# A hand-ordered attention and token-mixing kernel: the first batches' transfers in another sequence and every operation in a new order

## The chip, the cores and the metric

The kernel runs on one core of a Trainium2 chip. The core has TensorE (PE, matrix products into the eight banks of PSUM), VectorE (DVE), ScalarE (ACT), GpSimd (POOL, which cannot read PSUM) and SyncE (SP). Sixteen DMA engines move data between HBM and SBUF; POOL, SP and ACT each issue transfers on a queue of their own. The metric is the device time in microseconds, and smaller is better.

## The reference

Eight batches of eight heads, 576 positions, 64 columns a head; `p` has 32 rows a head. Everything arrives in float32.

```python
def sm_attn(qq, kk, vv):
    s = scale * np.matmul(qq, kk.transpose(0, 1, 3, 2))
    a = np.exp(s - np.max(s, axis=-1, keepdims=True))
    a = a / (np.sum(a, axis=-1, keepdims=True) + 1e-09)
    return np.matmul(a, vv)
p_packed = sm_attn(p, k, v)              # 32 rows attend to 576
x = sm_attn(q, p_packed, p_packed)       # 576 rows attend to 32
# heads side by side: x is (8, 576, 512)
W = scale2 * np.einsum("bsd,btd->bst", x @ w_q, x @ w_k)
out = np.maximum(np.einsum("bst,btd->bsd", W, x), 0.0) @ w_out
```

## The kernel before

**The order is written out by hand.** The text `SCHEDULE` (lines 11 to 60) is a list of some 650 items, and the last loop of the kernel emits them one after the other. An item `name@b` is one operation for batch `b`; behind it may stand the engine of an eviction or reduction (`s` ACT, `v` DVE, `g` POOL), the form of a product (`f` whole, `c` split into two halves of 64 columns), and behind a colon the PSUM bank or banks. Each engine takes its own items in the order of the list, and waits at each for what that item needs: its inputs, and the release of the bank or buffer that it overwrites. Nothing is reordered when the kernel runs. A transfer of POOL also waits until the transfer eight places earlier on that queue has landed, since its completion counter is one of eight used in turn.

**Loads.** `LQ`, `LK`, `LV` (line 149, POOL) bring q, k or v of one batch, 1.18 MB in float32, and cast it to bf16 on the way (576 KB). `PB` (line 180, POOL) brings `p` of all batches, `PF` (line 167, ACT) that of the first alone. The k of batch 0 comes on another path, in float32, through SP: `KA` and `KB` (line 170) bring half each into `k_f`, and `cA0` to `cB1` cast it on DVE or ACT. `cw0` to `cw3` (line 279) bring the two small mixing weights, `wo0`, `wo1` (line 288) the output weights. `id` builds the identity matrix for transposes on POOL.

**One batch, in the order of its data:**

- `kt0`, `kt1` (line 305, batch 0: `kf0` to `kf3`, line 258) transpose k by head on PE, `ke0`, `ke1` (batch 0: `kfe0` to `kfe3`) evict it into `kT`. `tp`, `lp` and `tr`, `lq0`, `lq1` do the same for `p`.
- `s0` (line 346) forms the first scores in three banks; `nm0` takes the maximum on DVE, `ex0` and `ex1` the exponentials on ACT (line 360) with their sums, `rc1` the reciprocal of these, `rm` (line 409, POOL) spreads it over a mask.
- `xt0`, `xt1` (line 377) transpose the exponentials, `xe0`, `xe1` evict them. `pv` (line 422) multiplies by v, `pp` (line 431) normalizes, `pt` and `pte` transpose and evict the packed rows.
- `qt0`, `qt1` with `qe0`, `qe1` do for q what `kt` does for k. `e0`, `e1`, `e2` (lines 471, 484) form the second scores. Their softmax goes one of two ways: batches 0 to 3 take `mn` (maximum), `ea` (it is added on PE, line 540) and `xa` (exponential), batches 4 to 7 `mx`, `sb` and `x0`. `sm0` sums, on DVE or, in five steps, on POOL, `rr0` inverts, `ml0` to `ml2` (line 576) multiply.
- `at0`, `at1` (line 596) transpose the weights, `ae0`, `ae1` evict them into `a2T`. `pq`/`pqe`, `wk`/`wke`, `wz`/`wkx`, `wq`/`wqe`, `g`/`ge`, `y`/`ye` are the small products of the mixing and their evictions.
- `m0`, `m1`, `m2` (lines 740, 765) mix, `r00` to `r11` and `r2` are the ReLUs, `o0` to `o4` (line 782) the output projection, `oe0` to `oe4` its evictions into `o_sb` and `ox`, and `st0` to `st2` (lines 812, 816, SP) the stores. `o_sb` has two slots for each half, so an eviction two batches later waits for the store.

`w1`, `w2` (line 204) multiply zeros into a bank, to keep PE occupied while it has nothing to do. Several batches are in work at a time: while PE projects batch `b`, the loads of batch `b + 4` and later arrive.

## Time and profile before

| | us |
|---|---|
| median of 3 runs | 118.99 (118.69 to 119.18) |
| the profiled execution | 119.33 |
| its span, first to last instruction | 117.6 |
| PE busy | 106.7 (91%) |
| DVE busy | 88.7 (75%) |
| ACT busy | 88.8 (76%) |
| POOL busy | 56.4 (48%) |
| filling products of PE (`w1`, `w2`) | 9.8 |

A row of the chain of waits or of the timeline gives a start and a length in microseconds, counted from the first instruction. PE's products are pipelined, so that the length of one is more than the distance to the next. A group's row gives the number of instructions, their busy time and mean in nanoseconds, and the idle time of the engine before them with what ended it. A row of DMA packets gives their number, the MB that they wrote, and their time as a share of sixteen engines.

### The profile page before, as it was taken

How to read it: one execution, taken by the hardware profiler on the slowest of the kernel's cores; microseconds unless marked ns; L12 is line 12 of the kernel's file. 1: busy time of each engine (PE TensorE's matmuls, PEld its weight loads, DVE VectorE, ACT ScalarE, POOL GpSimd, SP SyncE). 2: the span in 40 equal slices, each digit the busy share in tenths (PEclk: the TensorE clock that was granted, in tenths of full speed). 3: DMA queues.
4: the chain of work that ended last, by engine and by line, in shares of the span. 5: the costliest groups of instructions: out<-in, count | busy, mean ns of one | idle time of the engine just before them, and what ended most of it. 6: DMA issues, size and time to landing. Idle time of an engine off the chain costs nothing.

```text
span 117.6 us, 4918 instructions
## 1 busy us (share of the span) xinstructions
PE 106.7 (91%) x2134; PEld 70.1 (60%) x2134; DVE 88.7 (75%) x174; ACT 88.8 (76%) x172; POOL 56.4 (48%) x83
## 2 busy tenths in 40 slices
...
GB/s 62 373 206 207 209 207 208 189 207 208 208 209 205 209 207 209 207 209 207 209 206 211 220 329 241 212 198 377 380 165 112 66 8 233 308 89 307 381 355 117
DMA packets 18069, 25.47 MB, mean 217 GB/s; under 512 B 2176, under 2 KB 14720, under 8 KB 18048
## 3 DMA queue, kind: packets, MB, share of 16 engines
q0 software_dynamic: 13920, 14.49, 73.4%
...
## 4 chain that ended last, share of the span: by engine, by line
PE 59%; DMA 28%; ACT 3%; POOL 3%; issue 1%; DVE 1%; SPq 1%; POOLq 0%; ACTq 0%; DVEq 0%
PE psum L782 24%; DMA v_sb<-in_v_dram 20%; DMA out_dram<-o_sb 8%; PE psum L305 8%; PE psum L740 4%; PE psum L422 3%; PE psum L686 3%; PE psum L596 2%; PE psum L471 2%; PE psum L654 2%; PE psum L377 2%; PE psum L540 2%; PE psum L709 1%; ACT o_sb L136 1%; PE psum L438 1%
## 5 line engine op out<-in xcount | busy, mean ns | idle before, releaser
L782 PE MATMUL psum<-w_out,r 128*64 128x512 bf16 (+2 forms) x240 | 31.9, 373 | 0.5 <-ACT o_sb L136 0.5
L576 POOL TENSOR_TENSOR a<-e,rr 128x512 bf16<-128x512 f32 (+1 forms) x19 | 16.0, 866 | 9.1 <-DVE rr L572 4.1
L782 PEld LDWEIGHTS <-r 128*64 128x64 bf16 (+1 forms) x240 | 13.3, 109 | 11.0 <-issue 2.6
L136 ACT ACTIVATE o_sb<-psum 128x512 f32<-128x512 f32 (+1 forms) x25 | 14.4, 587 | 5.0 <-PE psum L782 4.2
L360 ACT ACTIVATE e1T<-psum,nmax 128x576 bf16<-128x576 f32 x16 | 11.7, 739 | 2.2 <-DVE nmax L356 2.2
L136 ACT ACTIVATE kT<-psum 128x1280 bf16<-128x1280 bf16 (+2 forms) x8 | 8.5, 1080 | 5.2 <-PE psum L305 4.9
L356 DVE TENSOR_REDUCE nmax<-psum 128x2 f32<-128x1152 f32 x8 | 10.8, 1355 | 2.1 <-PE psum L346 1.9
L305 PE MATMUL psum<-ident,q_sb 128*64 128x128 bf16 x288 | 10.4, 220 | 2.1 <-DMA q_sb<-in_q_dram 2.1
L136 ACT ACTIVATE r<-psum 128x512 bf16<-128x512 f32 x20 | 10.7, 610 | 0.8 <-PE psum L740 0.8
L204 PE MATMUL psum<-zero 128*64 128x512 bf16 (+1 forms) x39 | 9.8, 497 | 1.3 <-DVE zero L183 1.2
L305 PEld LDWEIGHTS <-q_sb 128*64 128x64 bf16 x288 | 8.5, 110 | 3.8 <-DMA q_sb<-in_q_dram 2.6
L565 POOL TENSOR_TENSOR rt<-e 128x576 f32<-128x576 f32 x4 | 5.7, 1416 | 8.6 <-ACT e L556 7.9
L305 PE MATMUL psum<-ident,k_sb 128*64 128x128 bf16 x252 | 9.1, 220 | 0.0
L149 POOL DMA_DIRECT2D v_sb<-in_v_dram x8 | 6.1, 767 | 5.7 <-DMA v_sb<-in_v_dram 2.9
L305 PEld LDWEIGHTS <-k_sb 128*64 128x64 bf16 x252 | 7.9, 110 | 1.0 <-issue 0.2
L138 DVE TENSOR_SCALAR r<-psum 128x512 bf16<-128x512 f32 x12 | 7.9, 683 | 0.6 <-PE psum L740 0.6
L149 POOL DMA_DIRECT2D q_sb<-in_q_dram x8 | 6.2, 779 | 4.6 <-PE psum L305 2.3
L142 DVE COPY qT<-psum 128x1280 bf16<-128x1280 bf16 (+1 forms) x10 | 7.5, 751 | 0.6 <-PE psum L305 0.4
L142 DVE COPY o_sb<-psum 128x512 f32<-128x512 f32 x8 | 5.5, 687 | 3.0 <-ACT o_sb L136 2.2
L136 ACT ACTIVATE e<-psum 128x512 bf16<-128x512 bf16 (+1 forms) x10 | 6.3, 639 | 1.1 <-PE psum L377 1.1
L149 POOL DMA_DIRECT2D k_sb<-in_k_dram x7 | 5.4, 770 | 3.6 <-DMA k_sb<-in_k_dram 3.0
L142 DVE COPY kT<-psum 128x1024 bf16<-128x1024 bf16 (+3 forms) x10 | 6.6, 662 | 0.6 <-PE psum L305 0.3
...
## 6 DMA issues: line engine op xcount, KB each, us to landing
...
```

What stands on the lines that cost most here:

```text
L136: nc.scalar.activation(dst, src, func, scale=scale)
L138: nc.vector.tensor_scalar(dst, src, 0.0, None, op0=MAX)
L142: nc.vector.tensor_copy(dst, src)
L149: nc.gpsimd.dma_start(t.rearrange("p g j d -> p g (j d)"), src[b].rearrange("(g h2) (sp j) d -> (h2 sp) g (j d)", h2=2, j=NJ),)
L204: nc.tensor.matmul(bank(ks[0])[r], zero[:, r], zero, start=True, stop=True, skip_group_check=True,)
L305: nc.tensor.transpose(tp[64 * g2:64 * g2 + 64, gp, :, 64 * (j - j0):64 * (j - j0) + 64], S_[b][src][:, gp + 2 * g2, order[j]], ident,)
L356: nc.vector.tensor_reduce(tile("nmax", [P, 2], fp32, b), S_[b]["s1"], axis=AX, op=MAX, negate=True)
L360: nc.scalar.activation(tile("e1T", [P, NJ, 2, 64], bf16, b)[:, :, h2], S_[b]["s1"][:, h2].rearrange("a (j s) -> a j s", j=NJ), EXP, bias=S ...
L565: nc.gpsimd.tensor_tensor(t, e[:, :, 0:16], e[:, :, 16:32], op=ADD)
L576: (nc.gpsimd if on == "g" else nc.vector).tensor_tensor(tile("a2", [P, NU, L], bf16, b)[:, r], S_[b]["e2"][:, r], S_[b]["rr"][:, r].to_bro ...
L740: nc.tensor.matmul(S_[b]["m", gp, h2], S_[b]["y"][r, 128 * gp:128 * gp + 128], S_[b]["wqT"][r, :], start=True, stop=True,)
L782: nc.tensor.matmul(ps[r, 0:w.stop - w.start], src[:, i, r], w_out[:, i, w], start=(i == 0), stop=(i == 3),)
```

## The change

The list is replaced as a whole; it has the same operations for every batch.

- At the start POOL issues `LQ@0` first, then `PB`, `LV@0`, `LK@1`, `LK@2`, and builds the identity only then; `LQ@1` and `LV@1` follow, and the weights `cw0` to `cw3` come behind `LV@1`. From `LK@3` on the loads have the order that they had. SP issues `KA` ahead of `KB`.
- 47 evictions and other operations move from ACT to DVE and 39 the other way; two multiplications move from DVE to POOL and one back. 26 products change between whole and split form, and most change their banks.
- The filling products are 28 pieces instead of 26, at other places of the list's first third.
- Among the operations of the middle, the order between batches changes by a few places throughout. The functions gain an operation that takes the three second scores of a batch in one step (`mn6`, `ea6`, `xa6`, `mx6`, `sb6`), which the new list doesn't use, and `e2` may be given no bank, which isn't used either.

The two lists, up to the point that the prediction follows, and the code:

```diff
-    id@0 PB@0 w1@0c:1 LQ@0 w1@0c:0 w1@0c:0 w1@0c:5 PF@0 LV@0 w1@0c:7 w1@0c:1 KB@0 LK@1 w2@0c:2
-    pfc@0s LK@2 w1@0c:1 cB0@0v KA@0 LQ@1 cB1@0v w1@0c:2 cA1@0s w1@0f:3 kf2@0:7 kfe2@0v w1@0c:3 cw1@0
-    kf3@0:1 cA0@0v tp@0:7 lp@0s w1@0f:6 kf0@0:0 kfe3@0v cw0@0 cw2@0 kfe0@0v kf1@0:3 kfe1@0s tr@0:76
-    lq1@0s cw3@0 s0@0:3 qt0@0:2 w1@0f:0 w1@0f:0 nm0@0 ex0@0 ex1@0 w1@0f:6 lq0@0s qt1@0:0 xt0@0c:4
-    xt1@0f:3 w1@0f:5 rc1@0 qe1@0v w1@0f:0 LV@1 rm@0 xe0@0v w1@0f:7 xe1@0s pv@0:3 qe0@0v w1@0c:0 pp@0
-    pt@0c:2 pte@0v e0@0c:4 kt1@1:1 ke1@1s mn0@0 e2@0:3 mn2@0 kt0@1:0 ke0@1v e1@0c:7 w1@0f:5 mn1@0
-    LK@3 LQ@2 ea2@0c LV@2 s0@1:0 ea0@0c LK@4 xa2@0 ea1@0f xa0@0 w1@0c:5 nm0@1 xa1@0 sm0@0v wo1@0
-    ex0@1 kt1@2:3 wo0@0 rr0@0 ml0@0v ex1@1 w1@0f:5 kt0@2:7 ke1@2s ke0@2s qt1@1:5 ml1@0v qe1@1v
-    xt0@1c:1 qt0@1:2 xt1@1c:0 LV@3 xe1@1v rc1@1 rm@1 ml2@0v at0@0f:4 qe0@1s w1@0f:3 s0@2:5 at1@0f:3
-    pq@0:2 xe0@1v ae0@0s pv@1:0 nm0@2 ae1@0s pqe@0s ex0@2 wk@0f:2 wz@0 pp@1 pt@1c:0 pte@1v LQ@3
-    wq@0:1 wkx@0 ex1@2 e1@1f:0 e0@1f:5 mn0@1 e2@1:7 mn2@1 wke@0s g@0f:2 ge@0v wqe@0s xt1@2f:4
-    xt0@2f:6 ea0@1c mn1@1 xe1@2s kt1@3:2 xe0@2v LK@5 xa0@1 ea2@1f xa2@1 ea1@1f xa1@1 ke1@3v pq@1:6
-    rc1@2 y@0:4 ye@0v pqe@1s kt0@3:1 ke0@3s rm@2 w1@0f:2 m1@0:45 sm0@1v rr0@1 ml1@1g r11@0s qt1@2:2
-    qe1@2s qt0@2:1 qe0@2v s0@3:5 pv@2:1 r10@0s ml0@1g nm0@3 m0@0:04 pp@2 pt@2f:1 r00@0v ex1@3
-    at0@1f:2 pte@2v ml2@1g ex0@3 r01@0v LQ@4 at1@1f:3 e1@2f:1 e0@2f:0 ae0@1s LV@4 mn1@2 ae1@1s LK@6
-    e2@2:6 mn2@2 kt0@4:7 kt1@4:4 ke1@4s LQ@5 ke0@4v mn0@2 wk@1f:3 wz@1 wke@1v wkx@1 wq@1:2 ea2@2c
-    rc1@3 rm@3 xa2@2 ea1@2c xa1@2 pq@2:7 pqe@2s wqe@1v ea0@2c xa0@2 s0@4:3 xt0@3f:6 xe0@3s xt1@3f:1
-    xe1@3s nm0@4 g@1f:2 sm0@2v rr0@2 o3@0f:7 LK@7 ml1@2g ge@1s ml2@2v ex1@4 ex0@4 rc1@4 o2@0f:0
-    ml0@2g o0@0c:2 oe0@0v LV@5 oe3@0s y@1:3 pv@3:5 LV@6 pp@3 ye@1s xt0@4f:1 xe0@4v m1@1:34 r11@1v
-    rm@4 oe2@0s m0@1:27 r00@1v qt0@3:0 qt1@3:5 r10@1s xt1@4c:4 r01@1s xe1@4s pt@3c:7 pte@3v LQ@6
-    at1@2f:2 m2@1f:1 qe1@3v at0@2f:7 qe0@3s o1@0f:4 ae0@2s e1@3f:3 e0@3f:6 r2@1v kt1@5:0 ae1@2v
-    pq@3:5 mn1@3 mn0@3 e2@3:2 mn2@3 oe1@0s pqe@3v ea1@3c kt0@5:7 LQ@7 ea0@3f ea2@3f ke1@5s xa1@3
-    ke0@5v xa0@3 wk@2f:4 wz@2 qt1@4:0 wq@2:3 wke@2v wkx@2 qe1@4v s0@5:5 g@2f:4 xa2@3 sm0@3g wqe@2s
-    qt0@4:0 ge@2s y@2:3 ye@2s nm0@5 ex0@5 ex1@5 qe0@4v pv@4:1 pp@4 o2@1c:3 rr0@3 m0@2:01 oe2@1s
-    m1@2:24 r11@2s ml0@3g pt@4f:5 r10@2s r01@2s pte@4v o1@1f:6 e1@4f:5 e0@4f:4 r00@2v at0@3f:0
-    ae0@3s oe1@1v mx0@4 xt0@5f:2 e2@4:6 xe0@5s kt0@6:1 pq@4:3 pqe@4s ke0@6s mx2@4 o0@1c:0 ml1@3g
-    kt1@6:2 oe0@1s mx1@4 ml2@3g sb2@4 st0@1 qt1@5:6 xt1@5f:1 at1@3f:0 sb1@4 sb0@4 x0@4 ae1@3s ke1@6v
-    s0@6:3 rc1@5 qe1@5v sm0@4g o4@1f:2 xe1@5s wk@3f:0 kt0@7:1 nm0@6 ex1@6 kt1@7:6 wz@3 rm@5 oe4@1v
-    ke0@7v wkx@3 ke1@7v qt0@5:2 wq@3:1 ex0@6 rc1@6 wke@3s qe0@5s pv@5:3 s0@7:5 rr0@4 pp@5 xt0@6f:2
-    pt@5f:3 ml0@4g wqe@3s nm0@7 xt1@6f:4 g@3f:0 LV@7 o3@1f:1 pte@5s e0@5f:3 ge@3v xe0@6s ml1@4g
-    o2@2f:2 e1@5f:0 ex0@7 xe1@6v ml2@4g at1@4f:4 mx0@5 ex1@7 at0@4f:5 sb0@5 oe3@1s y@3:6 mx1@5
-    e2@5:3 rm@6 st1@0 oe2@2s ye@3s ae0@4s xt0@7c:1 rc1@7 rm@7 mx2@5 sb1@5 sb2@5 ae1@4v xe0@7s
...
+    LQ@0 PB@0 KA@0 cA1@0v w1@0c:0 KB@0 w1@0c:0 w2@0f:1 LV@0 w1@0c:0 w2@0c:3 PF@0 pfc@0v w1@0c:7 LK@1
+    LK@2 id@0 w1@0c:3 w1@0f:7 cB0@0s cB1@0v kf1@0:6 kfe1@0v w1@0c:3 w1@0c:1 kf3@0:4 kfe3@0s kf2@0:7
+    w1@0f:5 cA0@0v kf0@0:6 tp@0:5 lp@0s kfe2@0v kfe0@0v s0@0:5 w1@0f:4 w1@0f:4 w2@0f:2 nm0@0 ex1@0
+    ex0@0 qt1@0:0 LQ@1 tr@0:34 lq0@0v xt0@0f:6 LV@1 xt1@0f:5 qt0@0:7 rc1@0 rm@0 xe1@0v xe0@0s pv@0:5
+    cw2@0 cw0@0 cw1@0 w1@0c:2 pp@0 w1@0c:2 pt@0f:5 cw3@0 w1@0f:2 w1@0c:2 pte@0v w1@0c:6 qe1@0s
+    qe0@0s e1@0c:5 mn1@0 kt0@1:0 kt1@1:2 lq1@0s LK@3 ea1@0c ke0@1v w1@0c:4 xa1@0 e2@0:7 e0@0c:6
+    ke1@1v s0@1:3 LQ@2 mn0@0 ea0@0c mn2@0 xa0@0 ea2@0f nm0@1 w1@0f:2 xa2@0 kt1@2:6 w1@0c:2 kt0@2:1
+    sm0@0v LV@2 rr0@0 ex1@1 ex0@1 xt1@1f:3 rc1@1 rm@1 ke1@2v qt0@1:2 qe0@1v ml1@0g xe1@1v qt1@1:4
+    w1@0f:6 ml2@0v xt0@1f:7 LK@4 xe0@1v ke0@2s s0@2:0 nm0@2 qe1@1s at1@0f:3 ex0@2 ml0@0g w1@0f:4
+    ex1@2 pv@1:5 pp@1 pq@0:7 pt@1c:5 ae1@0v at0@0f:4 pte@1v e0@1f:6 ae0@0v mn0@1 wo1@0 e1@1f:3 mn1@1
+    wo0@0 xt0@2f:2 LV@3 LQ@3 pqe@0s wk@0f:7 e2@1:5 wz@0 wkx@0 wke@0v ea0@1c kt1@3:0 LK@5 mn2@1
+    ke1@3v xe0@2s xa0@1 kt0@3:4 g@0f:7 ea2@1f xa2@1 pq@1:6 pqe@1s ea1@1c xa1@1 wq@0:0 wqe@0s
+    xt1@2c:5 xe1@2s rc1@2 ge@0v y@0:1 qt1@2:6 rm@2 ke0@3v ye@0v sm0@1v rr0@1 m0@0:43 r00@0v w1@0c:5
+    ml2@1g qe1@2s s0@3:0 ml1@1g nm0@3 r01@0s qt0@2:5 qe0@2s m1@0:67 r11@0s pv@2:3 ex1@3 pp@2 pt@2f:3
+    pte@2v ex0@3 at1@1f:4 r10@0v ml0@1g at0@1c:7 e0@2f:3 e1@2f:5 LQ@4 mn0@2 mn1@2 kt0@4:2 kt1@4:0
+    ke1@4v ea0@2f ae0@1s ae1@1s wk@1f:4 e2@2:7 wz@1 wke@1v mn2@2 ke0@4s ea1@2c s0@4:0 xt1@3c:6 xa0@2
+    ea2@2c xa1@2 wq@1:3 wkx@1 LV@4 xe1@3s xa2@2 xt0@3f:4 wqe@1s g@1f:5 ge@1s nm0@4 ex1@4 ex0@4
+    o2@0f:7 o3@0f:6 LK@6 oe3@0s xe0@3v rc1@3 sm0@2v rr0@2 pv@3:3 LQ@5 LK@7 LV@5 rm@3 oe2@0s pp@3
+    y@1:0 ye@1s pq@2:2 ml1@2v pqe@2s o0@0c:5 oe0@0s ml2@2v pt@3c:3 m1@1:64 r10@1v m0@1:02 rc1@4
+    at1@2c:1 qt0@3:5 r01@1s LV@6 r00@1s qt1@3:6 xt1@4f:0 r11@1s ae1@2v xt0@4c:2 ml0@2g qe0@3v
+    m2@1f:4 LQ@6 rm@4 pte@3s at0@2f:5 qe1@3v e0@3f:6 e1@3f:7 mn1@3 xe1@4s kt1@5:0 xe0@4s e2@3:3
+    kt0@5:2 mn0@3 ae0@2s ea1@3c r2@1s mn2@3 wq@2:5 ea0@3c ke0@5s xa1@3 ke1@5v xa0@3 wqe@2v wk@2f:4
+    wz@2 s0@5:0 wkx@2 ea2@3c xa2@3 o1@0c:7 wke@2v oe1@0s pq@3:4 qt1@4:5 nm0@5 qt0@4:3 qe1@4v pqe@3s
+    qe0@4v LQ@7 g@2f:7 pv@4:5 pp@4 ge@2s sm0@3g ex0@5 y@2:3 ye@2v ex1@5 o2@1f:7 oe2@1s rr0@3 ml2@3g
+    ml0@3g pt@4f:5 pte@4v m0@2:30 r00@2v m1@2:12 r10@2s e1@4f:4 mx1@4 r01@2s xt0@5f:5 e0@4f:7 xe0@5v
+    mx0@4 r11@2s sb1@4 rc1@5 ml1@3g o1@1f:6 oe1@1s kt1@6:0 e2@4:3 mx2@4 rm@5 ke1@6s sb0@4 kt0@6:2
+    pq@4:5 pqe@4s o0@1f:4 at0@3f:7 sb2@4 x0@4 qt0@5:3 qe0@5s sm0@4g ke0@6v s0@6:0 ae0@3v qt1@5:5
+    xt1@5f:7 qe1@5s oe0@1v st0@1 at1@3f:4 nm0@6 ex1@6 ae1@3v xe1@5v o4@1f:3 oe4@1v kt1@7:4 ke1@7v
+    rr0@4 ml0@4g ex0@6 rc1@6 kt0@7:6 ml2@4g ke0@7v ml1@4g wq@3:3 xt1@6f:0 pv@5:4 pp@5 xt0@6c:7
+    xe0@6v LV@7 st1@0 xe1@6s s0@7:0 nm0@7 wqe@3s pt@5c:4 pte@5s at0@4f:3 ae0@4s wk@3f:7 e2@5:4 wz@3
+    e0@5f:5 wke@3s ex1@7 o3@1f:6 ex0@7 mx2@5 e1@5f:3 wkx@3 rm@6 sb2@5 g@3f:7 ge@3s o3@2f:4 at1@4f:7
+    mx0@5 oe3@1s xt0@7f:0 o2@2f:6 mx1@5 sb1@5 oe3@2s xe0@7s ae1@4v sb0@5 y@3:3 ye@3v pv@6:1 wk@4f:5
...
@@ -476,9 +476,9 @@
         S_[b]["e", i] = ps.rearrange("s (u l) -> s u l", l=L)
 
     @op
-    def e2(b, ks):
-        S_[b]["e2bank"] = ks[0]
-        ps = bank(ks[0])[:, 0:128]
+    def e2(b, ks=None):
+        S_[b]["e2bank"] = ks[0] if ks else S_[b]["ebank", 0] + 2
+        ps = bank(S_[b]["e2bank"])[:, 0:128]
         for gp in range(2):
             for h2 in range(2):
                 nc.tensor.matmul(
@@ -490,7 +490,12 @@
 
     EU = EU + ((0, 32),)
 
+    def whole(b):
+        S_[b]["e", 6] = bank(S_[b]["ebank", 0], fp32, 3)[:, 0:NU * L].rearrange("s (u l) -> s u l", l=L)
+
     def units(i, t):
+        if i == 6:
+            return t
         if i >= 4:
             return t[:, 0:32].rearrange("s (x g) l -> s g x l", g=2)[:, i - 4]
         return t[:, EU[i][0]:EU[i][1]]
@@ -498,6 +503,8 @@
     def emax(i, b):
         if i == 3:
             S_[b]["e", 3] = bank(S_[b]["ebank", 0], fp32, 2).rearrange("s (u l) -> s u l", l=L)
+        if i == 6:
+            whole(b)
         nc.vector.tensor_reduce(units(i, tile("mx", [P, NU, 1], fp32, b)), S_[b]["e", i], axis=AX, op=MAX)
 
     def esub(i, b):
@@ -522,13 +529,15 @@
                             S_[b]["ppT"][r, h2, gp, 32 * g2:32 * g2 + 32], start=True, stop=True,
                         )
 
-    for i in range(6):
+    for i in range(7):
         if i < 2:
             ops[f"e{i}"] = lambda b, md, ks=None, i=i: scores(i, b, md, ks)
         ops[f"mx{i}"] = lambda b, i=i: emax(i, b)
         ops[f"sb{i}"] = lambda b, i=i: esub(i, b)
 
     def nmax2(i, b):
+        if i == 6:
+            whole(b)
         nc.vector.tensor_reduce(
             units(i, tile("mn", [P, NU, 1], bf16, b)), S_[b]["e", i], axis=AX, op=MAX, negate=True)
 
@@ -545,6 +554,13 @@
     def exps(i, b):
         nc.scalar.activation(units(i, tile("e2", [P, NU, L], fp32, b)), S_[b]["e", i], EXP, scale=scale)
 
+    def shifts(b, md):
+        for i in range(3):
+            shift(i, b, md)
+
+    ops["ea6"] = shifts
+    ops["mn6"] = lambda b: nmax2(6, b)
+    ops["xa6"] = lambda b: exps(6, b)
     for i in range(3):
         ops[f"mn{i}"] = lambda b, i=i: nmax2(i, b)
         ops[f"ea{i}"] = lambda b, md, i=i: shift(i, b, md)
```

34 lines of the change are left out of this document (17 added, 17 removed).

## The prediction

> **What bounds the kernel now.** I read the chain that ended last first, then a table by stages, then PE's waits, then POOL's issues and their landings.
>
> ```profile
> 14.62 12.44 DMA v_sb<-in_v_dram
> ...
> 38.94 1.20 PE psum L305 x36
> ...
> 41.74 0.60 PE psum L346 x8
> ...
> 64.04 9.37 DMA out_dram<-o_sb
> ...
> 73.48 0.61 ACT o_sb L136
> ```
>
> In this chain (start, length, what) LV@1, issued at 14.62, lands at 27.06, and pv@1 follows at 27.11, where the first stage of the next table ends. From there the chain is mostly PE's, but for a store that holds an o_sb slot until 73.4, for which the eviction at 73.48 waited.
>
> ```profile
> 14.48:27.11 12.63, 10.13 (x244) 7.22 (x245) 9.97 (x18) 7.98 (x13) 6.43 (x10) 1.00 1.29 203
> 27.11:38.94 11.83, 10.99 (x262) 8.19 (x262) 10.48 (x21) 10.53 (x23) 6.55 (x9) 1.00 1.22 207
> 38.94:58.50 19.56, 19.56 (x411) 13.51 (x412) 17.84 (x34) 16.76 (x35) 11.84 (x16) 1.00 1.21 208
> 58.50:74.20 15.70, 15.08 (x312) 10.90 (x311) 14.99 (x29) 13.90 (x28) 10.52 (x15) 1.00 1.18 239
> 74.20:113.30 39.10, 39.10 (x753) 24.01 (x752) 27.26 (x55) 31.65 (x59) 13.21 (x19) 1.00 0.66 225
> ```
>
> Columns: stage, length, then busy time of PE, weight loads, DVE, ACT, POOL, granted clock, DMA share, GB/s. The clock is 1.00 throughout, and the DMA engines are full (share over 1) up to 74 us. PE idles 2.5 us between pv@0 (14.48) and pv@1, 0.8 up to kt0@4 (38.94), nothing up to 58.5, 0.6 up to 74.2, and nothing in the 39 us behind that. PE's useful work is the same in both kernels (wide and split forms of a product take the same time in the chain), so the end moves by what happens before about 74 us: by when PE comes to a point, and how much of its list it has done by then. DVE and ACT are nearly as full as PE from 27 to 74 us.
>
> PE's own waits behind 38.94 are one row:
>
> ```profile
> PE psum L782 <- ACT o_sb L136: 0.5, 1, 0.5
> ```
>
> That is the projection which waited for the eviction of 73.48 to 74.09, which waited for the store's slot.
>
> **The change part by part.**
>
> *Loads.* The order of LQ, LV and LK is kept; PB falls behind LQ@0, and the four small cw transfers move from ahead of LV@1 to behind it. These rows are POOL's issues of PB, LQ@1, cw3, LV@1 and LK@4, then the times from issue to landing of LQ@1, cw3 and LK@4:
>
> ```profile
> 1.43 0.73 POOL L180 DMA_DIRECT2D p_b<-in_p_dram  x1
> ...
> 5.09 0.83 POOL L149 DMA_DIRECT2D q_sb<-in_q_dram  x1
> ...
> 11.13 0.61 POOL L279 DMA_DIRECT2D wqk<-in_moe_w_k_dram  x1 [2.27 <-DMA q_sb<-in_q_dram]
> 14.62 0.75 POOL L149 DMA_DIRECT2D v_sb<-in_v_dram  x1 [2.88 <-DMA v_sb<-in_v_dram]
> ...
> 24.33 0.75 POOL L149 DMA_DIRECT2D k_sb<-in_k_dram  x1
> ```
> ```profile
> DMA to landing us min/median/max: 18.2/18.2/18.2
> ```
> ```profile
> DMA to landing us min/median/max: 13.1/13.1/13.1
> ```
> ```profile
> DMA to landing us min/median/max: 14.6/14.6/14.6
> ```
>
> LQ@1 lands at 23.3, cw3 at 24.2, LK@4 at 38.9: without the weights ahead of it LV@1 comes 0.9 earlier, at 26.1, and the weights at 27.1, before pq@0 wants them. LK@3 and all that follow have the same bytes ahead of them as before, so they land when they did: LK@4 at 38.9, where kt0@4 stood ready in the old kernel. POOL's issue now waits for the transfer eight places earlier, as LV@1 did above (2.88 for LV@0), but always with two loads or more in the queue; I cost that at nothing, as cover is some 6 us.
>
> *The start.* id goes behind five issues, so LQ@0 is issued at about 0.73 instead of PB at 1.43. ident is then ready at about 5, still ahead of its first use (k_f lands at 5.1). Whether the earlier issue gains or harms depends on how it shares with the two k_f transfers of SP:
>
> ```profile
> q1 hardware_dynamic: 91, 0.21, 108.7%
> ```
>
> This is the whole of what moved from 5.0 to 5.5 (packets, MB, share of the engines): SP's queue alone. PB, issued at 1.43, had moved nothing 4.1 us later, with the engines full of k_f. With the same lag LQ@0 moves at 4.8. By then some 0.3 to 0.4 MB of k_f are left (0.21 of it in this half microsecond), 0.9 us for k_f alone. Shared evenly, k_f's second half lands up to 0.9 later; queued behind, not at all. I take +0.5, and for the range 0 and what an even share from 2.6 us on would cost (rivals). The Trainium skill's page DMA: Bandwidth & Descriptors (Issuing engines are not separate DMA queues) says that DMAs of several engines interleave on the same 16, so that starting one earlier saves only issue time; by it too the earlier start gains no bandwidth, and the row of full engines agrees.
>
> *Front, batch 0.* The rows are a cast of k_f behind its second landing and two kT evictions:
>
> ```profile
> 6.67 0.49 DVE L142 CAST k_sb<-k_f 128x640 bf16<-128x640 f32 x1
> 7.08 0.42 DVE L142 COPY kT<-psum 128x512 bf16<-128x512 bf16 x1
> 7.73 0.49 DVE L142 COPY kT<-psum 128x640 bf16<-128x640 bf16 x1 [0.23 <-PE psum L258]
> ```
>
> DVE now runs cB1, kfe1 and then cA0 after the second landing, though cA0's data came at 5.1: 6.67 + 0.49 + 0.42 + 0.49 = 8.07, then kf0's ten transposes (7.21 to 7.68 in the old order, between these rows) and kfe0, 0.49: s0@0 at about 9.3 where the old order could have it at 8.9, +0.4. pv@0, then, is held by its own evictions instead of LV@0: about 14.6, +0.1. Behind it there is a gain: rm@0 no longer stands behind LV@1's issue on POOL (14.62 to 15.37, then rm@0's own time), so pp@0 is 0.7 earlier, and batch 0's scores with it. Through kt@1, s0@1, nm0@1 and ex@1 this shrinks, since xt1@1 waits for both exponentials: nm0@2 starts at 26.35 as before and pv@1 at about 26.9 (-0.2), with at0@0 and pq@0 (0.34 us) not yet done. The 0.9 of LV@1 is thus mostly not used: pv@1's other input, xe0@1, is there at 26.1 at best, and PE has s0@2 and at1@0 ahead of it.
>
> *27 to 42 us, where the order decides.* Between nm0@2 and pp@2 DVE loses xe0@2 and qe0@2 and gains ae1@0, ae0@0, wke@0, ke0@3 and r00@0. Means from the groups by shape:
>
> ```profile
> L142 DVE COPY qT<-psum 128x1024 bf16<-128x1024 bf16 x5 | 3.4, 688 | 0.4 <-PE psum L305 0.4
> ...
> L142 DVE COPY kT<-psum 128x1024 bf16<-128x1024 bf16 x4 | 2.8, 692 | 0.3 <-PE psum L305 0.3
> ...
> L142 DVE COPY a2T<-psum 128x768 bf16<-128x768 bf16 x4 | 2.2, 550 | 0.7 <-PE psum L599 0.7
> L142 DVE CAST wk<-psum 128x256 bf16<-128x256 f32 x5 | 2.1, 418 | 0.2 <-ACT e L546 0.2
> ...
> L142 DVE COPY e<-psum 128x640 bf16<-128x640 bf16 x4 | 1.9, 482 | 0.0
> ```
>
> 0.55 (ae1, 768 columns) + 0.42 (ae0, taken as wk's) + 0.42 (wke) + 0.69 (ke0) + 0.69 (the ReLU, taken as qT's copy) - 0.48 (xe0) - 0.69 (qe0) = +1.6 us, in a stage where DVE idles 11.83 - 10.48 = 1.35. It is full, and pp@2 ends 0.2 to 0.6 later; I take 0.4 (37.7 for 37.3). nm0@3 ahead of it is late as much, ACT's ex1@3 and ex0@3 follow, and kt0@4, written into banks that ex0@3 reads, waits for them to 39.35 instead of LK@4 at 38.9. ACT then has ae0@1, ae1@1 and ke0@4 before s0@4: at about 41.5, where the old kernel had it at 41.6. By then the new list lacks wq@1, ea2@2 and pq@2 (0.44 + 0.06 + 0.11 = 0.6 us of PE, start to start). Net +0.5, and a full PE does not win that back.
>
> *42 to 76 us.* Followed through with the same durations, PE finds its inputs in time; small waits at pv@4 and s0@7 add 0.2. The wait of 0.5 on that eviction goes: o3@2 uses bank 4, which PE wants only at m0@3, two us later. But oe0@1 is late on DVE, so st0@1 and st1@0 are issued about 1 us later than 64.04 and the slot comes free at 74 to 75; y@3 is what waits then, by 0 to 1. I take -0.3 in all (-0.5 to +0.7).
>
> *Behind 76 us* PE has the same products; evictions move between DVE and ACT, which have 11.8 and 7.4 us to spare there (39.10 less 27.26 and 31.65). I take 0; the last evictions and stores are the same pieces as before.
>
> Sum: +0.5 (start) +0.5 (27 to 42) -0.3 = +0.7 us on the profiled execution's 119.33. That lies 0.34 above the median of 118.99; against the median it is 119.7.
>
> **The rivals.**
>
> *The loads run ahead (faster).* If the engines have room at the start, all of the stream, LK@4 too, lands earlier by what the first issue gains, 1.43 - 0.73 = 0.7; with half the forecast's gain behind 42 us (-0.3), and DVE keeping up, the time is 118.99 - 1.0 = 118.0. For it: what PE does up to 58 us hangs on landings. Against: PB's 4.1 us of waiting on full engines, and DVE's full stage, which does not follow the loads. It decides if kt0@4 starts before 38.6.
>
> *The parts cancel (no change).* k_f is not disturbed, and the 0.5 lost up to 42 us is paid by the 0.5 of that one wait: 119.0.
>
> *LQ@0 breaks into k_f (clearly slower).* While both queues have work they take turns:
>
> ```profile
> q1 hardware_dynamic: 244, 0.93, 61.6%
> q0 software_dynamic: 301, 0.33, 48.2%
> ```
>
> From 67 to 71 stores and loads move about packet for packet. If LQ@0's packets don't wait as PB's did, but come while k_f has only begun, at about 2.6, then nearly 1 MB of k_f shares half and half from there, the second half lands 2.4 later, and the chain s0@0, nm0@0, ex, pv@0, pp@0, s0@1, pv@1 moves with it: 118.99 + 0.2 + 2.4 = 121.6. It decides from a k_f landing behind 7.5. Against it: PB had its descriptors written at 2.16 and took no turn until 5.5. The Trainium skill's page DMA: Bandwidth & Descriptors (Queues, rings and completion order) has each DMA engine go round its queues packet by packet; by that rule this rival is what happens, the rows of 67 to 71 agree with it, and those of PB don't.
>
> **How the numbers follow.** A run tells 0.5% (0.6 us) from no change. The forecast's case (start and DVE cost, little gained back, 119.2 to 120.6) has 0.40, of which 0.13 lies within 0.5%; cancelling 0.20; loads ahead 0.24; LQ@0 into k_f 0.16. So faster 0.24, same 0.20 + 0.13 = 0.33, slower 0.27 + 0.16 = 0.43. The range goes from 118.1, within the faster case, to 121.3, near the end of the slowest; some 0.1 is left out on either side. The forecast's own range is 119.2 to 120.6.
>
> **What would show it.** LV@1 landing at 26.1 with pv@1 still at 26.7 or later, behind s0@2 and at1@0; k_f's second landing between 6.6 and 7.5; DVE without idle time from 26 to 38; kt0@4 behind ex0@3 and not behind LK@4; s0@4 at 41.3 to 42.3; no wait of L782 on an o_sb eviction about 74, but one of L725 there. The prediction is wrong if pv@1 starts before 26.4 and kt0@4 with LK@4's landing, if that landing itself moves from 38.9, or if PE has a wait of over 0.5 us behind 76, where I expect none.

## The result and the profile after

The changed kernel takes 119.9 us (median of 14 runs, 118.94 to 120.15) where before takes 119.01 (14 runs on the same chip, 118.57 to 120.44): a ratio of 1.0059, with a 95% interval of 1.003 to 1.0087. It is slower by about 0.6%, and the 119.7 of the prediction lies 0.2 below it. The profiled execution took 119.78, with a span of 118.0; that of before took 119.33 and 117.6. The granted clock was 0.992 to 1.000 in the changed kernel's 14 runs, the short ones and the long ones alike, so it is not what spreads them.

At four points TensorE has done the same set of operations in both kernels: ahead of `kt0@4` (but for `e2@2`, 0.06, which the changed kernel still has to do there), `o2@1`, `pv@6` and `y@6`/`y@7`. Between them the lengths can be compared directly. These are the tables of stages with the boundaries at these points, first before, then the changed kernel. The columns are the stage, its length, and then busy time and instructions of PE, weight loads, DVE, ACT, POOL, the granted clock, the DMA share and GB/s.

```profile
38.94:56.72 17.78, 17.78 (x396) 12.75 (x397) 16.69 (x32) 14.98 (x31) 10.81 (x13) 1.00 1.21 208
56.72:75.12 18.40, 17.78 (x336) 12.01 (x333) 16.91 (x34) 16.61 (x34) 11.63 (x18) 1.00 1.19 235
75.12:101.60 26.48, 26.48 (x626) 17.64 (x624) 19.71 (x41) 23.85 (x43) 13.13 (x18) 1.00 0.64 207
```
```profile
39.46:57.56 18.10, 17.95 (x419) 12.91 (x417) 16.35 (x29) 16.05 (x35) 10.77 (x14) 1.00 1.21 208
57.56:75.10 17.54, 17.54 (x325) 11.67 (x325) 17.10 (x35) 15.13 (x31) 10.60 (x16) 1.00 1.18 236
75.10:102.11 27.01, 26.60 (x631) 17.77 (x632) 22.84 (x50) 21.36 (x37) 13.75 (x19) 1.00 0.65 212
```

The changed kernel comes to `kt0@4` 0.52 later (39.46 for 38.94), loses 0.32 more up to `o2@1`, takes 0.86 less up to `pv@6`, where both are level (75.10 and 75.12), and loses 0.53 behind that. The sum is +0.51, and the time is +0.45.

PE's waits behind 27 us, in the changed kernel:

```profile
PE psum L438 <- DVE pp L431: 1.5, 2, 0.9
PE psum L422 <- issue: 0.4, 1, 0.4
```

The first row is `pt@1` and `pt@2`, which wait for DVE's `pp`. The wait of 0.5 on an o_sb eviction is gone, as forecast. The second row is new. "Issue" means that PE waited for nothing that the trace shows, and it lies behind 76 us, where I expected nothing. First the changed kernel, then before at the same operation:

```profile
83.91 0.28 PE L422 MATMUL psum<-v_sb,e 64*64 64x128 bf16 x7
84.59 0.60 PE L422 MATMUL psum<-v_sb,e 64*64 64x128 bf16 x29 [0.41 <-issue]
```
```profile
84.42 0.70 PE L422 MATMUL psum<-v_sb,e 64*64 64x128 bf16 x36
```

In the changed kernel `pv@7` stops after 7 of its 36 products.

The front, in the chain of waits, the last rows ahead of the full stage of DVE:

```profile
25.46 0.77 DVE a L592
26.25 0.48 DVE e L142
26.72 0.95 DVE nmax L356
```

LV@1 landed at 26.29 (before 27.07) and PE began `pv@1` at 26.87 (before 27.11), so LV@1 no longer holds PE. What stands ahead of `nm0@2` is a multiply of the softmax, `ml2@0` (line 592, which is 576 in before). The timeline shows it on DVE beside one of POOL, then the same place in before:

```profile
25.11 1.05 POOL L592 TENSOR_TENSOR a<-e,rr 128x512 bf16<-128x512 f32 x1
25.38 0.94 DVE L592 TENSOR_TENSOR a<-e,rr 128x128 bf16<-128x128 f32 x1
```
```profile
25.75 0.27 DVE L576 TENSOR_TENSOR a<-e,rr 128x128 bf16<-128x128 f32 x1
```

The same work takes 0.94 instead of 0.27 and ends at 26.32, 0.16 after POOL's multiply. In the old order the multiplies of batch 0 are all on DVE and meet none on POOL. The experiments show how much of the loss such meetings make.

### The profile page after: what moved, and what is told of

Its sections match the earlier page's. It is cut to its first block, busy times and chain, and to the rows that moved or that the text cites. A ratio compares the mean times of both kernels' runs of the same rounds, so it can differ in the third digit from the quotient of the medians.

```text
span 118.0 us, 4914 instructions
## 1 busy us (share of the span) xinstructions
PE 106.3 (90%) x2132; PEld 69.2 (59%) x2132; DVE 92.0 (78%) x184; ACT 84.3 (71%) x161; POOL 57.4 (49%) x84
## 4 chain that ended last, share of the span: by engine, by line
PE 70%; DVE 15%; DMA 5%; ACT 4%; issue 3%; SPq 0%; DVEq 0%; ACTq 0%
PE psum L798 26%; PE psum L305 9%; DVE nmax L356 5%; DMA k_f<-in_k_dram 5%; PE psum L377 4%; PE psum L471 3%; PE psum L422 3%; PE psum L756 3%; PE psum L612 3%; ACT e1T L360 3%; PE psum L702 3%; PE psum L670 2%; PE psum L346 2%; PE psum L725 1%; DVE mn L541 1%
## 5 line engine op out<-in xcount | busy, mean ns | idle before, releaser
L798 PE MATMUL psum<-w_out,r 128*64 128x512 bf16 (+3 forms) x224 | 31.9, 374 | 0.0
L592 POOL TENSOR_TENSOR a<-e,rr 128x512 bf16<-128x512 f32 (+1 forms) x20 | 17.1, 877 | 8.8 <-DVE rr L588 6.9
L798 PEld LDWEIGHTS <-r 128*64 128x64 bf16 (+1 forms) x224 | 12.7, 108 | 9.5 <-issue 0.8
L136 ACT ACTIVATE r<-psum 128x512 bf16<-128x512 f32 x22 | 12.0, 605 | 1.5 <-PE psum L756 1.3
L136 ACT ACTIVATE qT<-psum 128x1280 bf16<-128x1280 bf16 (+1 forms) x10 | 11.3, 1144 | 1.8 <-PE psum L305 1.8
L409 POOL TENSOR_TENSOR rm<-mask,rrec 128x256 f32<-128x256 f32 x8 | 5.0, 619 | 9.0 <-DVE rrec L370 8.9
L142 DVE COPY kT<-psum 128x1280 bf16<-128x1280 bf16 (+3 forms) x13 | 8.9, 694 | 0.5 <-PE psum L258 0.2
L555 ACT ACTIVATE e<-psum 128x512 f32<-128x512 f32 (+1 forms) x12 | 5.7, 492 | 3.0 <-PE psum L549 3.0
L377 PE MATMUL psum<-ident,e1T 128*128 128x128 bf16 (+1 forms) x94 | 6.5, 221 | 1.3 <-ACT e1T L360 1.3
L541 DVE TENSOR_REDUCE mn<-psum 128x16 bf16<-128x512 f32 (+1 forms) x12 | 6.2, 551 | 1.7 <-PE psum L471 1.5
```

The costliest lines, as they stand in the source:

```text
L136: nc.scalar.activation(dst, src, func, scale=scale)
L142: nc.vector.tensor_copy(dst, src)
L377: nc.tensor.transpose(tp[r, j - j0, :], S_[b]["e1T"][:, j].rearrange("a h s -> a (h s)")[:, r], ident,)
L541: nc.vector.tensor_reduce(units(i, tile("mn", [P, NU, 1], bf16, b)), S_[b]["e", i], axis=AX, op=MAX, negate=True)
L555: nc.scalar.activation(units(i, tile("e2", [P, NU, L], fp32, b)), S_[b]["e", i], EXP, scale=scale)
L592: (nc.gpsimd if on == "g" else nc.vector).tensor_tensor(tile("a2", [P, NU, L], bf16, b)[:, r], S_[b]["e2"][:, r], S_[b]["rr"][:, r].to_bro ...
```

## The experiments

Twelve kernels, in three groups of four; each group shared its chip and its runs of before. The medians of before were 118.89, 118.95 and 118.88.

**The changed order with the old loads**

```diff
-    LQ@0 PB@0 KA@0 ... LK@2 id@0 ... LQ@1 ... LV@1 ... cw2@0 cw0@0 cw1@0 ... cw3@0
+    id@0 PB@0 LQ@0 KA@0 ... LK@2 ... LQ@1 cw1@0 cw0@0 ... cw2@0 cw3@0 LV@1 ...
```

> The changed kernel's order with the load sequence of before (id and PB first, the four cw transfers ahead of LV@1). If the load sequence sets little, as the prediction has it: k_f's second landing goes back from 7.03 to about 6.6, s0@0 from 9.84 to about 9.4, LV@1 lands at 27.1 instead of 26.29, pv@1 starts at 27.1 to 27.3 instead of 26.87, kt0@4 still behind ex0@3 at 39.4 to 39.6, and the end is within 0.2 of the changed kernel. Rival, the disturbed start is carried to the end: then kt0@4 is back at 39.0 and the end comes 0.4 to 0.5 earlier than in the changed kernel. The pause of 0.41 inside pv@7 should be there again at the same matmul, since TensorE's instructions are the same, if it hangs on the instructions; if it was chance, it is gone.

Measured: 120.21, ratio 1.0101 (1.0062 to 1.0139). LV@1 landed at 26.52 and `pv@1` began at 26.85; `kt0@4` came at 39.50, as in the changed kernel. Against that execution of the changed kernel the loads are worth nothing so far, as I had it; two further kernels, below, say otherwise. But then the kernel lost 1.08 at one place that neither theory had named. This is its timeline there, and the same place in the changed kernel:

```profile
46.43 0.80 POOL L149 DMA_DIRECT2D v_sb<-in_v_dram  x1 [1.32 <-DMA q_sb<-in_q_dram]
46.60 2.47 DVE L592 TENSOR_TENSOR a<-e,rr 128x512 bf16<-128x512 f32 x2
47.25 1.06 POOL L592 TENSOR_TENSOR a<-e,rr 128x512 bf16<-128x512 f32 x1
48.92 0.41 PE L612 MATMUL psum<-ident,a 128*64 128x128 bf16 x8 [1.01 <-DVE a L592]
```
```profile
46.56 0.88 DVE L592 TENSOR_TENSOR a<-e,rr 128x512 bf16<-128x512 f32 x2
47.15 0.81 POOL L149 DMA_DIRECT2D v_sb<-in_v_dram  x1 [1.51 <-DMA q_sb<-in_q_dram]
47.80 0.41 PE L612 MATMUL psum<-ident,a 128*64 128x128 bf16 x8
47.98 1.06 POOL L592 TENSOR_TENSOR a<-e,rr 128x512 bf16<-128x512 f32 x1
```

The row of DVE is `ml1@2` and `ml2@2`. The new list has moved `ml1@2` from POOL to DVE. POOL began to issue LV@6 0.17 before DVE began, with its own multiply `ml0@2` right behind, and DVE stood until POOL's multiply was over: 2.47 instead of 0.88. (A start 0.01 and 0.09 behind that of the issue, `ml2@2` in the two traces of the changed kernel, cost nothing.) POOL issues LV@6 0.29 after LQ@3 has landed (46.14 here, 46.86 in the changed kernel), so a landing that was 0.7 earlier turned it. The pause in `pv@7` was not there: it began at 85.07 and ran through.

**Three evictions from DVE to ACT**

```diff
-    ... ae1@0v ... ae0@0v ... wke@0v
+    ... ae1@0s ... ae0@0s ... wke@0s
```

> The changed kernel with ae1@0, ae0@0 and wke@0 on ScalarE instead of VectorE, 1.4 us off VectorE's full stage between 27 and 38 us. Theory (late pp@2, nm0@3 and ex0@3 make kt0@4 late): nm0@3 ends before 37.2, pp@2 ends before 37.5, kt0@4 is bound by LK@4's landing at 38.9 instead of 39.46, and the end comes 0.3 to 0.5 earlier, 119.4 for 119.9. Rival, ScalarE is as full there (10.17 of 12.59 us) and ex0@3 waits behind the three evictions: kt0@4 at 39.4 or later, the end the same or up to 0.4 later. Second rival, kt0@4 comes earlier and the gain goes into the wait of g@2 and pv@4 at 56 us: the end within 0.2.

Measured: 120.81, 1.0149 (1.0113 to 1.0186); `kt0@4` came at 41.02. The first rival holds, and more strongly than I had it. ACT has no room either, and the late evictions hold banks that PE wants:

```profile
PE psum L438 <- DVE pp L431: 1.3, 2, 0.9
PE psum L471 <- ACT a2T L136: 0.8, 1, 0.8
PE psum L450 <- ACT e L555: 0.4, 1, 0.4
PE psum L756 <- DVE y L140: 0.3, 1, 0.3
```

It does not tell whether `kt0@4`'s lateness comes from DVE; the six traces that are compared further down tell more.

**Some 50 more instructions ahead on TensorE**

```diff
-    ... xt0@0f:6 ... xt1@0f:5 ... pt@0f:5 ... xt1@1f:3 ... xt0@1f:7 ... xt0@2f:2
+    ... xt0@0c:6 ... xt1@0c:5 ... pt@0c:5 ... xt1@1c:3 ... xt0@1c:7 ... xt0@2c:2
```

> The changed kernel with six transposes of the first 33 us (xt0 and xt1 of batches 0 and 1, xt0@2, pt@0) in split form instead of wide: about 50 more instructions ahead of everything else on TensorE, no other work. If the pause of 0.41 inside pv@7 (nothing waited for, 7 matmuls at 83.91, then 29 from 84.59) comes from the arrival of instructions, it moves to another instruction, shrinks or goes, and the end is 0 to 0.4 earlier. If it belongs to pv@7 and its data, it stays ahead of the eighth matmul of pv@7 and the end is within 0.1. The split forms themselves are expected to cost nothing up to 38 us (0 to 0.2).

Measured: 121.90, 1.0212 (1.0158 to 1.0266). The end came later, not earlier. `ml2@2` stood for 1.57 instead of 0.28 (a wait of 0.58 at `at1@2`), and with the pauses the last eviction ended 0.87 later than in the changed kernel (114.98 for 114.11). Another 1.08 lies behind it: the end came 4.97 after the last eviction, and 3.9 after it in each of the other 13 traces. A load of code at 112.51, which no other trace has so late, stood beside the last stores; whether it held them was not tried. For the question asked, the pause left `pv@7`, and two others appeared, at 41.39 (0.19) and 54.87 (0.34), both inside `wz`:

```profile
54.31 0.22 PE L681 MATMUL psum<-a2T,pqk 128*64 128x64 bf16 x2
54.87 0.22 PE L681 MATMUL psum<-a2T,pqk 128*64 128x64 bf16 x2 [0.34 <-issue]
```

The pause therefore does not belong to `pv@7` or its data.

**The changed kernel again, and with one multiply put back**

```diff
-    y@1:0 ye@1s pq@2:2 ml1@2v pqe@2s
+    y@1:0 ye@1s pq@2:2 ml1@2g pqe@2s
```

> The changed kernel once more, for its time and a second trace. The theory of the shared port (a multiply of the softmax, ml1@2 or ml2@2 on VectorE, that starts while GpSimd is at work stands still until GpSimd is done: 0.68 became 2.27 with the old loads, 0.28 became 1.57 in the shifted one) has the usual time of 119.9 come from there: the trace of a run at 119.8 to 120.2 shows ml1@2 or ml2@2 at 1.2 us or more near 47 us, a wait of 0.5 to 1.0 at at1@2 (line 612) and no pause inside pv@7. Rival, the pause of 0.41 inside pv@7 is what the usual time has: then it is there again and the multiplies take 0.68 and 0.28.

> The changed kernel with one operation put back where before has it: the multiply ml1@2 on GpSimd instead of VectorE. If the changed kernel's usual time comes from VectorE's multiplies that stand still behind GpSimd at 47 us, the time falls to that of its rare quick runs, 118.9 to 119.4, with no run near 120. If it does not (the pause inside pv@7, or something spread over the list), it stays at 119.7 to 120.1.

Measured: the changed kernel 119.87 (12 runs, 1.0052, interval 1.0018 to 1.0086), five of them from 119.07 to 119.44 and seven from 119.74 to 120.17. With `ml1@2` put back 119.27 (12 runs, 1.0019, interval 0.9985 to 1.0053): ten from 118.98 to 119.50, two at 119.96 and 120.15. One operation on another engine is worth 0.6 of the median, and most of the upper group goes. The trace that was taken of the changed kernel is one of 119.22: in it the multiplies of batch 2 take 0.68 and 0.28, and the pause in `pv@7` is there (0.26 in the row of waits). So the pause is not what separates the two groups, and no trace caught the changed kernel itself with a multiply of batch 2 standing; that this makes its upper group is inferred from the kernels around it. The upper group has at least one other source: the first trace, of 119.78, belongs to it, has the same 0.68 and 0.28, and is 0.56 longer than the second one mainly because `nm0@2` began 0.50 later.

**No multiply of batch 2 on DVE**

```diff
-    ... ml1@2v pqe@2s o0@0c:5 oe0@0s ml2@2v
+    ... ml1@2g pqe@2s o0@0c:5 oe0@0s ml2@2g
```

> The changed kernel with ml1@2 and ml2@2 on GpSimd, so that no multiply of batch 2 on VectorE can start while GpSimd works. If the standing still of these multiplies makes the changed kernel's runs near 120 (7 of 12 in the last comparison; 2 of 12 with ml1@2 alone put back, where ml2@2 still took 0.76), all runs lie between 118.9 and 119.5. If something else makes them, a share of the runs stays at 119.8 to 120.2.

Measured: 119.43, 1.0035 (1.0011 to 1.0058). Six of 12 runs lie from 118.99 to 119.33 and the others spread from 119.53 to 120.03, so the expectation (all below 119.5) failed for half of the runs, and the multiplies of batch 2 are not all that makes long runs. The trace, the longest of these runs, shows a pause of PE that no other kernel had there:

```profile
48.21 0.44 PE L305 MATMUL psum<-ident,q_sb 128*64 128x128 bf16 x9
49.30 0.33 PE L305 MATMUL psum<-ident,q_sb 128*64 128x128 bf16 x5 [0.65 <-issue]
```

**Two neighbours exchanged in before**

```diff
-    ... ml1@2g ge@1s ml2@2v ex1@4 ex0@4 rc1@4
+    ... ml1@2g ge@1s ex1@4 ex0@4 rc1@4 ml2@2v
```

> Before's kernel with two neighbours on VectorE exchanged: rc1@4 (0.16 us) runs ahead of the multiply ml2@2, so that ml2@2 starts at about 45.85 instead of 45.52, behind GpSimd's ml1@2 (45.64 to 46.72) instead of ahead of it. All other engines keep their order. Theory of the shared port: ml2@2 takes 1.1 (until ml1@2 ends and its own time) or 2.1 (until GpSimd's next multiply, ml0@2, ends too) instead of 0.29, pp@3 and xe0@4 are as much late, and the time is 0 to 1.2 longer, most likely 0.6, as pp@3 has some slack. Rival, the two engines do not disturb each other: ml2@2 takes 0.29 and the time is unchanged within 0.1.

Measured: 119.39 (12 runs, 119.05 to 119.55, against a median of 118.88; the ratio of 1.0023 has an interval of 0.9995 to 1.0051, so the loss in time is not settled). The mechanism is. First before, then the exchange:

```profile
45.52 0.29 DVE L576 TENSOR_TENSOR a<-e,rr 128x128 bf16<-128x128 f32 x1
45.64 2.09 POOL L576 TENSOR_TENSOR a<-e,rr 128x512 bf16<-128x512 f32 x2 [2.47 <-ACT e1T L360]
```
```profile
45.27 2.10 POOL L592 TENSOR_TENSOR a<-e,rr 128x512 bf16<-128x512 f32 x2 [2.46 <-ACT e1T L360]
45.31 1.15 DVE L592 TENSOR_TENSOR a<-e,rr 128x128 bf16<-128x128 f32 x1
```

Starting 0.12 ahead of POOL, the multiply takes 0.29; starting 0.04 behind, it takes 1.15 and ends at 46.46, when POOL's first multiply is over (46.30). It did not wait for the second one.

**The new loads alone, and the new order alone**

The first is before's list with the new sequence of loads. The second is the list of the old-loads kernel with `ml1@2` and `ml2@2` on POOL.

```diff
-    id@0 PB@0 w1@0c:1 LQ@0 ... LK@2 ... LQ@1 ... cw1@0 ... cw0@0 cw2@0 ... cw3@0 ... LV@1 rm@0
+    LQ@0 PB@0 w1@0c:1 ... LK@2 id@0 ... LQ@1 LV@1 ... rm@0 cw2@0 cw0@0 cw1@0 cw3@0
```
```diff
-    ... ml1@2v ... ml2@2v
+    ... ml1@2g ... ml2@2g
```

> Before's order with the changed kernel's load sequence (LQ@0 and PB first, id behind LK@2, the four cw transfers behind LV@1 and rm@0). By the prediction's steps: k_f's second landing 6.64 becomes 7.0 to 7.2, s0@0 is 0.1 to 0.5 later, LV@1 lands at 26.2 for 27.06, pv@1 starts at 26.4 to 26.9 instead of 27.11, and kt0@4 is still bound by LK@4's landing at 38.9, so that the end is within 0.2 of before (118.8 to 119.1). Rival, the late k_f is carried through to the end: +0.4, 119.4. Rival, LV@1's 0.9 is carried: kt0@4 before 38.6, 118.5 or less.

> The changed kernel's order with before's load sequence, and ml1@2 and ml2@2 on GpSimd so that the 1.15 us which the same kernel lost at ml1@2 does not cover the rest. The trace of that kernel had kt0@4 at 39.50 (before 38.94) and the ledger without the 1.15 gives 120.2 - 1.15 = 119.05. Prediction's theory (late ex0@3 makes kt0@4 0.5 late, the wait on the o_sb eviction at 74.1 goes, -0.3): 119.1 to 119.4. Rival, order and loads together lose more than each alone: then this one is at before's 118.9 and the changed kernel without collisions at 119.2.

Measured: the loads alone 120.98 (120.73 in the trace), 1.0179 (1.0134 to 1.0224), a miss of all three theories. In the old list PE transposes `p` (`tr@0`) ahead of `s0@0`, and `p` now lands at 10.78 instead of 7.97:

```profile
10.82 1.08 PE L234 MATMUL psum<-ident,p_b 128*64 128x128 bf16 x32 [2.59 <-DMA p_b<-in_p_dram]
11.74 0.60 PE L346 MATMUL psum<-kT,pT_bd 128*64 128x512 bf16 x6
```

`s0@0` is 2.8 late, `pv@0` 2.7, `s0@1` 2.0, and 2.0 (against the exchange of two neighbours, whose front is before's) are still there at `pv@1` and `kt0@4`. The new list has `tr@0` behind `s0@0`, so it needs `p` later; the two parts of the change belong together. LV@1 landed at 25.83 here and served nobody.

The order alone took 119.84 (10 runs, 119.15 to 120.30), 1.0072 (1.0043 to 1.0101): the first theory's 119.1 to 119.4 was too little. Its trace has the old loads and no multiply of batch 2 on DVE, but `ml2@0` still on DVE:

```profile
24.66 1.05 POOL L592 TENSOR_TENSOR a<-e,rr 128x512 bf16<-128x512 f32 x1
...
25.21 1.14 DVE L592 TENSOR_TENSOR a<-e,rr 128x128 bf16<-128x128 f32 x1
25.65 0.81 POOL L149 DMA_DIRECT2D k_sb<-in_k_dram  x1
```

The kernel without a multiply of batch 2 on DVE, above, differs from this one in the loads alone. Its trace at the same place:

```profile
24.55 1.05 POOL L592 TENSOR_TENSOR a<-e,rr 128x512 bf16<-128x512 f32 x1
25.85 0.80 POOL L149 DMA_DIRECT2D k_sb<-in_k_dram  x1 [0.25 <-DMA v_sb<-in_v_dram]
```
```profile
25.13 0.63 DVE L592 TENSOR_TENSOR a<-e,rr 128x128 bf16<-128x128 f32 x1
```

With the new loads the issue of LK@4 waits for the landing of LV@1, eight places earlier, and does not follow POOL's multiply at once; `ml2@0` ends 0.60 earlier, and `kt0@4` comes at 38.89 instead of 39.48. The medians are 119.43 and 119.84, on the same chip; the runs overlap (118.99 to 120.03 against 119.15 to 120.30). So in the new order the new loads are worth about 0.4, and in the old order they cost about 2.

**Lists put together from both, inconclusive.** Three kernels took the changed kernel's order in one stretch and before's in the others, with banks renamed at the joints: the front up to 38.8 us, and twice the stretch from 58 to 75 us.

```diff
+    (front)    the new list up to LQ@4, then the old from ae0@1s; kt0@4:7 to :2, kt1@4:4 to :0, wk@1f:3 to :4
+    (stretch)  the old list up to pp@4, the new from o2@1f up to ye@3v, the old from pv@6
```

> The changed kernel's loads and order up to 38.8 us (e0@2 and LQ@4), then before's order, with three banks renamed at the joint. At the joint TensorE has done the same operations in both. The traces put the changed kernel 0.52 behind there (kt0@4 at 39.46 for 38.94). If a full TensorE does not win it back: 119.4 to 119.7, +0.4 to +0.7 on before. If what follows has slack (evictions and weights that waited are now there): within 0.2 of before. A stretched multiply (ml2@2 on VectorE near 46 us, over 1 us) would add up to 1.

> Before's kernel up to pp@4 (58 us) and from pv@6 (75 us) on, with the changed kernel's order in between; the banks behind the joint are renamed. Between these two points TensorE has done the same set of operations in both kernels, and the changed one takes 0.86 less for it (before 56.72 to 75.12, changed 57.56 to 75.10). Theory, the stretch alone makes the gain (the wait of 0.5 on the o_sb eviction at 74.1 and one of 0.24 on a weight at 60 go): pv@6 starts at 74.2 to 74.4 and the end comes 0.7 to 0.9 earlier than before, 118.2 for 119.0. Rival, the stretch was only quick because its inputs were 0.84 late on TensorE's side and had time to get ready: started 0.84 earlier, the same waits come back (y@3 or o3@2 behind an eviction that waits for a store's slot), and the gain is 0 to 0.3.

> The same as the kernel with the changed kernel's stretch from 58 to 75 us, with other banks at its beginning: there o2@1 was written into a bank that exponentials of s0@5 still read, and waited 1.46 us at 58.07; behind 75 us oe2@2 is now on VectorE. Without that wait the stretch begins at 56.7 as in before. Theory, the stretch alone is worth the 0.77 (58.07 to 75.70 took 17.63, where before took 18.40): the time is 118.1 to 118.5. Rival, what begins 0.84 earlier meets the waits of before again (an eviction behind a store's slot about 74): 118.7 to 119.2.

Measured: the front 120.19, 1.0086 (1.0056 to 1.0116); the stretch 120.41, 1.0113 (1.0072 to 1.0153), and with other banks 120.58, 1.0119 (1.0074 to 1.0165). In each a wait at the joint hides the answer, because PE writes into a bank that is still being read. These are the waits of the front behind 38 us, then those of the stretch from 50 to 90:

```profile
PE psum L346 <- ACT e L555: 1.1, 1, 1.1
```
```profile
PE psum L798 <- ACT e1T L360: 1.5, 1, 1.5
```

The second set of banks traded the one wait for three (0.7, 0.3 and 0.3). They show that one bank asked for too early costs over a microsecond (1.1 and 1.5). That the stretch is worth 0.86 by itself stays open.

## Why the prediction was nearly right, and where its reasons were not

**The start, +0.5: failed.** LQ@0 was issued at 1.25, not 0.73, and it moved its first packet at 5.59, not 4.8. In all 14 traces POOL's queue moves its first packet between 5.48 and 5.77, whichever transfer stands first in it. k_f's second landing moved from 6.64 to 7.03, as the step had it, but not because of LQ@0: over the six traces with the old sequence it lies from 6.50 to 7.02, over the eight with the new one from 6.43 to 7.03. `s0@0` came at 9.84, as the 9.3 and +0.5 of the steps give, yet at `s0@1` 0.10 of the 0.91 was left, and `pv@1` was 0.24 early. Between `pv@0` and `s0@1` there was slack that I did not count; the loads alone show its size, about 0.7 of 2.7. A loss ahead of it costs only what exceeds that.

**LV@1's 0.9 is not used: held.** It landed 0.8 earlier (26.29), and `pv@1` started at 26.87, the figure of the prediction. What I did not see is its use for POOL: LK@4's issue now waits for it, which keeps that issue away from `ml2@0` (two kernels that differ in the loads alone were compared above).

**27 to 42 us, +0.5: right in size in this execution, half right in cause.** `pp@2` ended at 37.93; I had 37.7 for 37.3. DVE's full stage from `nm0@2` to `pp@2` lasts 10.87 from start to start instead of 10.52: +0.35, where I took 0.4. The other 0.3 is `nm0@2`, which I had at 26.35 "as before" and which came at 26.65, behind the `ml2@0` that stood. `ml2@0` lost 0.67, and half of that was made up, since it began 0.37 earlier than in before.

When `ml2@0` ended can be read on POOL. It ended 0.16 behind POOL's `ml1@0`, which runs straight behind `rm@1` and the issue of LV@2, and that issue waits for LQ@1. LQ@1 landed at 23.49 in the changed kernel and at 23.00 in its second trace:

```profile
23.78 0.74 POOL L149 DMA_DIRECT2D v_sb<-in_v_dram  x1 [3.00 <-DMA q_sb<-in_q_dram]
```
```profile
23.28 0.74 POOL L149 DMA_DIRECT2D v_sb<-in_v_dram  x1 [2.35 <-DMA q_sb<-in_q_dram]
```

From the start of this issue to `nm0@2` it is 2.87 in each of the four traces of this order with the new loads in the table below, and 3.34 and 3.39 in the two with the old ones, where `ml2@0` stood longer. So the +0.5 at `kt0@4` belongs to an execution in which one landing was late; in the three others with the new loads it comes at 38.89 to 38.96, against 38.94 in before's trace and 38.41 to 38.83 in three other traces that have before's front.

`kt0@4` was not held by `ex0@3`, as I had it: PE went through the work ahead of it without a pause from `pt@2` on, and `pt@2` had waited 0.90 for `pp@2`. In the six traces of this order with `ae1@0`, `ae0@0` and `wke@0` on DVE and the front's products whole, `kt0@4` is 12.81 behind `nm0@2` each time:

```
kernel            ml2@0   nm0@2   kt0@4   stop in pv@7   other stop   time
changed            0.94   26.65   39.46       0.62           -        119.78
changed, again     0.68   26.15   38.96       0.47           -        119.22
ml1@2 put back     0.77   26.13   38.94       0.40           -        119.19
ml1, ml2 on POOL   0.63   26.08   38.89       0.34          0.86      120.03
order alone        1.14   26.67   39.48       0.48           -        119.74
old loads          1.14   26.69   39.50       0            1.08       120.34
```

(`ml2@0` is its length; a stop in `pv@7` is the step from its start to the next operation's, less the 0.60 that it takes undisturbed; the two other stops are those of `qt1@3` and `at1@2`, worked out in the same way.) The time less `kt0@4` and less the stops is 79.70 to 79.94 in all six. These numbers are then nearly the whole difference among the traces of this order. In before the time less `kt0@4` is 80.39, so the new order does win 0.5 to 0.7 behind 39 us where nothing stops it, and its front and its stops cost it again.

**42 to 76 us, -0.3: too small.** From `kt0@4` to `pv@6` the changed kernel gains 0.54 (0.86 less 0.32). The wait on the o_sb eviction went (0.50 of it; in the two other traces of the old order that wait was 0.2), and `y@3` waited for nothing, where I gave it 0 to 1. The wait at `pv@4` that I had in the 0.2 is 0.3 as PE's steps show it, behind an eviction of q on DVE (55.90, 0.84, in the chain). A wait of 0.24 on a POOL multiply at 59.97 in before is gone as well.

**Behind 76 us, 0: failed.** It is +0.53, and all of it the stop inside `pv@7`. This is the condition that I had named for being wrong, a wait of PE behind 76 us, though the row of waits shows 0.41, and only the step from product to product, 0.62 longer than undisturbed, is over 0.5.

**What no step had.** The change moved `ml1@2` from POOL to DVE, and `ml0@0` and `ml1@0` the other way. I priced these moves by engine time only. In every trace, a multiply with both inputs in SBUF that began on DVE while POOL was multiplying stood at least until that multiply of POOL's was over. `ml1@7` is a case that no step of mine had either: 0.98 instead of 0.69 in each trace of the new order, without a wait of PE behind it. The Trainium skill's page SBUF — State Buffer (Who interferes with whom) says just this: a VectorE instruction with two SBUF inputs contends with a GpSimd instruction that reads SBUF, and whichever begins first keeps the shared ports while the other blocks fully. The traces agree: 0.27 against 0.94 for `ml2@0`, 0.29 against 1.15 in the exchange. By that rule the steps would have had another +0.3 at `nm0@2`, and a rival of up to +1.1 at `at1@2`, where `ml1@2` on DVE is close to POOL's `ml0@2` (1.06). Two multiplies that stood do not fit it so simply: with the old loads and with 50 more instructions they began ahead of POOL's multiply, 0.17 and 0.47 into an issue of POOL's.

So +0.5 +0.5 -0.3 stood against +0.52 -0.54 +0.53: the total agreed by luck, because a loss that was absorbed was replaced by one that I had excluded. Nor is the account that of the kernel, but of one pair of executions: with the changed kernel's second trace in its place it begins with +0.02 at `kt0@4`, and the time is 119.22. The usual time is 0.9 above before, while the two profiled executions differ by only 0.45, since that of before was 0.32 above the median of its 14 runs and that of the changed kernel 0.12 below. One multiply put back takes 0.6 off the median.

What stays open: what decides from run to run whether a multiply of batch 2 stands or TensorE stops, why LQ@1 landed 0.5 later in one execution than in another, and how the usual 0.9 divides among the multiplies, the stops and the late landings. The version that these readings point to, the changed order with `ml2@0` also kept clear of POOL's multiplies, was not tried.
